# A four-tap shift filter moved wholly to TensorE, with 64-row tile pairs and a new written order

## The chip, the cores and the metric

The kernel runs on one core of a Trainium2 chip. The metric is the device time of one execution in microseconds (us). Before the change it is 241.32 us, the median of three runs (241.05 to 241.69). A separate execution was recorded by the hardware profiler; its span, from the first to the last instruction, is 238.8 us.

## What is computed

Two layers, each a long-convolution mixer (A) and an MLP (B), on 2048 positions of 512 channels in bf16:

```python
def _A_ref(q, k, v, shift_k, ssm_k, ssm_D):
    for t in range(ks):                       # ks = 4
        k_shift = k_shift + k_pad[:, t:t + S, :] * shift_k[:, ks - 1 - t][None, None, :]
    kv = k_shift * v
    ...
    y_f = kv_f * kf_f[None, :, :, :]          # rfft of kv and of ssm_k, both padded to 2S
    y = irfft2(y_f)[:, 0, :S, :]
    y = y + kv * ssm_D[None, None, :]
    return q * y
...
x = A_q
x = x + _A_ref(_layernorm(x), A_k, A_v, A_shift_k, A_ssm_k, A_ssm_D)
x = x + _B_ref(_layernorm(x), B_w1, B_b1, B_w2, B_b2)     # layernorm, gelu MLP, 512 -> 1376 -> 512
x = x + _A_ref(_layernorm(x), A_k, A_v, A_shift_k, A_ssm_k, A_ssm_D)
x = x + _B_ref(_layernorm(x), B_w1, B_b1, B_w2, B_b2)
```

The convolved signal y depends on k, v and the filters, not on x, so the kernel computes it once and uses it in both layers. The mixer A then costs only a layernorm, a product and a sum per layer.

## The kernel before, in words

**Stages.** The sequence is seen as 128 rows of 16 positions; the partition is the row. The Fourier transform is done by matmuls in two stages. "ht" transposes ssm_k (L528), "h1" is its first stage (L545, L547 in `stage1`), "h2" its second (L558, `stage2`). "fir" is the shift filter on k and the product with v, for four chunks of 128 channels; "x1" is the first stage for the result (`stage1` again), "x2" the second (L651, `products`), whose output is multiplied with the spectrum H (L450 by way of `tt`). "i1" (L674, `inverse1`) and "i2" (L731, `inverse2`) go back. Channels are cut in two halves (`PARTS`), and x2, i1 and i2 run per half, tagged `_0` and `_64`.

TensorE (PE) writes every tile to PSUM. `evac` (L453) copies it out, on ScalarE (ACT) or VectorE (DVE). A tile takes two of the eight PSUM banks in these stages, so four are open at a time. Between h2 and the products, 16 DMA copies swap partitions of H into a second array HS (L439, `ar<-ar`).

**The shift filter before.** Two chunks (0 and 1, `PE_CH`) go by `shift_pe`: 16 transposes of k (L589), an eviction into KT, then matmuls with diagonal tap matrices (L606; per chunk four groups of seven, 128 x 128 weights and 128 to 512 moving columns), and the product with v straight from PSUM (L613, on DVE). The other two chunks go by `shift_tt`: eight DVE instructions of 128 x 2048 each (four multiplications with the taps, three additions, the product with v; L450). For them k has three halo columns loaded by two further DMAs, and the taps are spread over partitions by a matmul (L511). The eight diagonal matrices are made on GpSimd (POOL, L520).

**The mixer and the MLP.** Layer 0 goes in nine blocks (`BLOCKS0`: 1, 1, then seven of 2 slices of 128 positions), layer 1 in four of 4. Per slice DVE takes statistics (L754, L756), normalizes (L768), multiplies with y and adds (L450); POOL computes the inverse root (L760, L762). The second layernorm's result z is transposed, by TensorE for the first two slices (L814) and by DMA for the others (L807), and goes through the MLP: L827 with gelu on ACT (L832), L860 (L849 for the last slice) with the sum on DVE (L864).

**The order.** Each engine runs a fixed queue. `Prog` collects operations with what they read and write; three tables written out by hand give the order of all operations (`ORDER`), which of the two engines takes an eviction (`SECOND`), and the PSUM banks (`BANKS`). `sync` derives the waits: an operation waits for its last producer, for readers of what it overwrites, and for the users of its PSUM banks. All loads, the HS copies and the DMA transposes but a few small ones are issued from one queue (SP), in order: a DMA whose wait is unmet holds back those behind it.

**Places.** One SBUF array `ar` is cut by hand. Before, the x1 output GX lies in R_4, where the h1 output G had been; k lies in R_K, and the MLP weight W1 and the table T2 are loaded over k later.

## Time and profile before

| | |
|---|---|
| median of three runs | 241.32 us |
| profiled execution, span | 238.8 us |
| runs minus span | 2.5 us |
| PE busy | 226.2 us (95%), 2312 instructions |
| DVE busy | 171.6 us (72%) |
| ACT busy | 138.3 us (58%) |
| POOL busy | 41.3 us (17%) |
| granted TensorE clock | 1.000 |
| DMA | 27.40 MB, 37035 packets |

Busy time is the time in which an engine had an instruction of the kernel in work. Matmuls are pipelined, so PE's duration of one (219 ns for 128 columns) is longer than the distance between two (about 56 ns); distances are read from the timeline. "Idle before, releaser" says how long an engine stood still ahead of a group and whose end let it go. Shares over the whole span mix stages that have different limits; here the first 83 us (Fourier stages) and the rest (mixer and MLP) are to be read apart.

### The profile page before, as it was taken

How to read it: one execution, taken by the hardware profiler on the slowest of the kernel's cores; microseconds unless marked ns; L12 is line 12 of the kernel's file. 1: busy time of each engine (PE TensorE's matmuls, PEld its weight loads, DVE VectorE, ACT ScalarE, POOL GpSimd, SP SyncE). 2: the span in 40 equal slices, each digit the busy share in tenths (PEclk: the TensorE clock that was granted, in tenths of full speed). 3: DMA queues.
4: the chain of work that ended last, by engine and by line, in shares of the span. 5: the costliest groups of instructions: out<-in, count | busy, mean ns of one | idle time of the engine just before them, and what ended most of it. 6: DMA issues, size and time to landing. Idle time of an engine off the chain costs nothing.

```text
span 238.8 us, 5555 instructions
## 1 busy us (share of the span) xinstructions
PE 226.2 (95%) x2312; PEld 151.6 (63%) x2332; DVE 171.6 (72%) x359; ACT 138.3 (58%) x225; POOL 41.3 (17%) x77
## 2 busy tenths in 40 slices
PE   7987989886999999999999999999999999999995
PEld 3875778875899886766766667644444444444543
DVE  0979999999999999999887999693793312030035
ACT  2598799999999995642754444342782042454100
POOL 2179000000013444041230310400220200000000
PEclk9999999999999999999999999999999999999999
DMA  6999949999960003111122022240013021310024
GB/s 241 364 342 383 383 148 253 249 272 309 379 227 0 3 0 68 26 23 31 37 47 44 0 48 44 45 88 3 0 22 66 3 44 31 101 44 3 0 71 148
DMA packets 37035, 27.40 MB, mean 115 GB/s; under 512 B 19506, under 2 KB 29969, under 8 KB 37010
## 3 DMA queue, kind: packets, MB, share of 16 engines
q1 hardware_dynamic: 36446, 26.91, 37.8%
q8 instruction: 18, 0.29, 0.5%
q10 hardware_dynamic: 564, 0.14, 0.4%
q14 instruction: 7, 0.06, 0.1%
HBM read 16.82 MB, written 2.10 MB: 79 GB/s over the span
## 4 chain that ended last, share of the span: by engine, by line
PE 77%; ACT 9%; DMA 4%; DVE 4%; SPq 3%; issue 3%; ACTq 0%
PE ps L860 31%; PE ps L827 30%; ACT ar L453 9%; PE ps L674 5%; PE ps L731 3%; SPq L439 3%; PE ps L545 3%; DMA ar<-in_A_ssm_k_dram 2%; DVE ar L453 2%; DMA ar<-ar 2%; PE ps L528 1%; PE ps L606 1%; PE ps L849 1%; DVE sm L754 1%; PE ps L589 1%
## 5 line engine op out<-in xcount | busy, mean ns | idle before, releaser
L832 ACT ACTIVATE ar<-ps,sm 128x256 bf16<-128x256 f32 (+4 forms) x143 | 64.7, 525 | 72.5 <-PE ps L827 68.1
L827 PE MATMUL ps<-ar 128*128 128x256 bf16 (+4 forms) x568 | 84.2, 297 | 0.2
L860 PE MATMUL ps<-ar 128*128 128x512 bf16 (+1 forms) x329 | 79.0, 379 | 0.6
L453 ACT ACTIVATE ar<-ps 128x1024 bf16<-128x1024 f32 (+1 forms) x81 | 72.5, 1057 | 9.0 <-PE ps L511 4.5
L827 PEld LDWEIGHTS ps<-ar 128*128 128x128 bf16 (+1 forms) x572 | 52.9, 100 | 29.8 <-ACT ar L832 0.5
L450 DVE TENSOR_TENSOR ar<-ar 128x512 bf16<-128x512 bf16 (+3 forms) x106 | 63.6, 634 | 2.0 <-DMA ar<-in_A_k_dram 1.3
L860 PEld LDWEIGHTS ps<-ar 128*128 128x128 bf16 (+1 forms) x341 | 33.1, 98 | 34.3 <-ACT ar L832 0.3
L864 DVE TENSOR_TENSOR ar<-ar,ps 128x512 bf16<-128x512 bf16 x31 | 20.6, 680 | 47.3 <-PE ps L860 47.3
L754 DVE BATCH_NORM_STATS2 sm<-ar 128x6 f32<-128x512 bf16 (+1 forms) x68 | 42.8, 647 | 0.1
L768 DVE TENSOR_SCALAR ar<-ar,sm 128x512 bf16<-128x512 bf16 x64 | 25.0, 407 | 7.8 <-POOL sm L762 5.2
L760 POOL TENSOR_SCALAR sm<-sm 128x2 f32<-128x2 f32 (+2 forms) x26 | 6.0, 232 | 93.9 <-DVE sm L756 93.3
L762 POOL TENSOR_TENSOR sm<-sm 128x2 f32<-128x2 f32 (+2 forms) x26 | 21.6, 832 | 2.2
L545 PE MATMUL ps<-ar 128*64 128x128 bf16 x512 | 17.1, 221 | 1.4 <-issue 0.8
L545 PEld LDWEIGHTS ps<-ar 128*64 128x64 bf16 x512 | 14.9, 110 | 3.2 <-issue 1.0
L674 PE MATMUL ps<-ar 128*128 128x128 bf16 x256 | 15.0, 220 | 0.6 <-ACT ar L453 0.6
L674 PEld LDWEIGHTS ps<-ar 128*128 128x128 bf16 x256 | 14.7, 114 | 0.8 <-ACT ar L453 0.8
L453 DVE CAST ar<-ps 128x1024 bf16<-128x1024 f32 x11 | 13.0, 1212 | 0.3 <-PE ps L558 0.3
L651 PE MATMUL ps<-ar 128*128 128x64 bf16 x256 | 9.8, 194 | 3.2 <-ACT ar L453 2.7
L453 DVE COPY ar<-ps 128x2048 bf16<-128x2048 bf16 (+1 forms) x8 | 8.2, 1024 | 6.4 <-PE ps L528 6.3
L651 PEld LDWEIGHTS ps<-ar 128*128 128x128 bf16 x256 | 8.2, 98 | 4.7 <-ACT ar L453 3.9
L756 DVE BATCH_NORM_AGGREGATE sm<-sm 128x2 f32<-128x6 f32 (+1 forms) x64 | 9.9, 171 | 0.3
L558 PE MATMUL ps<-ar 128*128 128x128 bf16 x128 | 8.6, 220 | 0.8 <-ACT ar L453 0.8
(34 smaller groups left out, 78.1 us busy)
## 6 DMA issues: line engine op xcount, KB each, us to landing
ar<-tab_s SPq DMA_DIRECT2D x16, 256.0 KB, 9.6
ar<-ar SPq DMA_DIRECT2D x16, 256.0 KB, 4.2
ar<-in_A_ssm_k_dram SPq DMA_DIRECT2D x4, 512.0 KB, 5.3
ar<-in_A_k_dram SPq DMA_DIRECT2D x8, 256.0 KB, 7.6
ar<-in_A_v_dram SPq DMA_DIRECT2D x8, 256.0 KB, 9.6
ar<-in_A_q_dram SPq DMA_DIRECT2D x4, 512.0 KB, 7.9
out_dram<-ar SPq DMA_DIRECT2D x7, 256.0 KB, 2.1
ar<-in_B_w_dram SPq DMA_DIRECT2D x1, 1376.0 KB, 12.6
```

The lines of the kernel that those rows point to most:

```text
L450: return P.op(eng, lambda e: e.tensor_tensor(o, a, b, op), reads=[a, b] + list(more), writes=[o])
L453: f = {ACT: lambda e: e.activation(dst, src(), AF.Copy), DVE: lambda e: e.tensor_copy(dst, src())}
L545: r = e.matmul(Q(tl, 64 * ri, 64, i * 128, [1, 128]), w, m, start=True, stop=True)
L651: r = e.matmul(Q(tl, 0, 128, i * pitch, [1, n]), w, m, start=True, stop=True)
L674: r = e.matmul(Q(tl, 0, 128, i * 128, [1, 128]), w, m, start=q == 0, stop=q == 1)
L754: P.op(DVE, lambda e, sj=sj, x=x: e.bn_stats(sj, x), reads=[x], writes=[sj])
L762: P.op(POOL, lambda e: e.tensor_tensor(r, v, hf, ALU.pow), reads=[v, hf], writes=[r])
L768: P.op(DVE, lambda e: e.tensor_scalar(o, x, m, r, ALU.subtract, ALU.mult), reads=[x, m, r], writes=[o])
L827: r = e.matmul(Q(tl, 0, rows, 0, [1, w]), a, m, start=dk == 0, stop=dk == 3)
L832: P.op(ACT, lambda e, dst=dst, tl=tl, rows=rows, bias=bias, w=w: e.activation(dst, Q(tl, 0, rows, 0, [1, w]), AF.Gelu_apprx_tanh, bias=bia ...
L860: r = e.matmul(Q(tl, 0, 128, 0, [1, 512]), ins[fc][0], ins[fc][1], start=fc == 0, stop=fc == 10)
L864: P.op(DVE, lambda e, x=x, tl=tl: e.tensor_tensor(x, x, Q(tl, 0, 128, 0, [1, 512]), ALU.add), reads=[x], writes=[x], tile=tl)
```

## The change

1. All four chunks of the filter go by matmul. `shift_tt`, the halo loads, the spreading of taps by a matmul and its two evictions are gone. KT has four buffers, k no halo.
2. The filter's matmuls take 64 rows each, in pairs: rows 0 to 63 and 64 to 127 of the same KT column block, each with its own diagonal (64 wide) and its own PSUM bank. Per chunk there are two halves of 22 matmuls with 64 to 256 moving columns, and two DVE products of 512 elements per half instead of one of 1024. The four diagonals are each made by one POOL multiplication of 128 x 256.
3. i1 likewise: per tile 32 matmuls of 64 rows and 64 columns instead of 16 of 128 and 128, and two evictions of 512 elements instead of one of 1024. The S2 table is permuted so that the pairs of d lie in one half of the partitions, and the table U halves.
4. GX of the first channel half is put where k was (R_K); the second half stays in R_4. W1 and three of the four T2 pieces, which lie over R_K, are loaded after x2 of the first half.
5. `ORDER`, `SECOND` and `BANKS` are new throughout: which engine evicts which tile, and the order on all queues, the DMA issues too. The loading of the gelu table comes after ACT's seventh eviction, so that a first table is loaded ahead of the first.

```diff
-PE_CH, PO_CH = (0, 1), ()
...
-    R_KT = (R_7, R_7 + 2080)
+    R_KT = (R_7, R_7 + 2080, R_6, R_6 + 2080)
...
-    R_GX, R_Z = R_4, R_4
+    R_Z = R_4
+    GX = {PARTS[0][0]: R_K, PARTS[1][0]: R_4 + 128 * PARTS[1][0]}
...
-    for i in range(4 * NPE):
-        o, t = A(0, 128, R_DG + i * 128, [1, 128]), M(0, 128, M_TAP + i, [1, 1])
-        P.op(POOL, lambda e, o=o, t=t: e.tensor_scalar(o, IDN, t, None, ALU.mult), reads=[IDN, t], writes=[o])
+    for c in range(4):
+        o = A(0, 128, R_DG + 256 * c, [64, 4], [1, 64])
+        tt(o, A(0, 128, R_FO, [0, 4], [1, 64]), A(0, 128, R_TC + 4 * c, [1, 4], [0, 64]), ALU.mult, POOL)
...
-        for a8 in range(2):
+        for a0 in (0, 8):
             tl = Tile(2)
             ins = []
-            for g in (2 * a8, 2 * a8 + 1):
-                for b in (0, 1, 2, 3, -1, -2, -3):
-                    j0, j1 = max(0, -b), min(3, 3 - b)
-                    ins.append((b, 512 * (g % 2) + 128 * max(b, 0), 128 * (j1 - j0 + 1),
-                                A(0, 128, R_KT[i] + (4 * g + b) % 16 * 130 + (2 if 4 * g + b >= 0 else 1), [1, 128]),
-                                A(0, 128, R_DG + (i * 4 + j0) * 128, [1, 128 * (j1 - j0 + 1)])))
+            for a in (0, 4, 1, 2, 3, 5, 6, 7, -1, -2, -3):
+                j0, j1 = max(0, -a), min(3, 7 - a)
+                k = R_KT[c] + (a0 + a) % 16 * 130 + (2 if a0 + a >= 0 else 1)
+                for r in range(2):
+                    ins.append((a, 512 * r + 64 * (a + j0), 64 * (j1 - j0 + 1), A(64 * r, 64, k, [1, 128]),
+                                A(64 * r, 64, R_DG + 256 * c + 64 * j0, [1, 64 * (j1 - j0 + 1)])))
...
-    def shift_tt(i):
-        c = DV_CH[i]
-        eng = POOL if c in PO_CH else DVE
-        acc, tmp = [A(0, 128, o, [128, 16], [1, 128]) for o in (R_TMP + 2048 * i, R_KV + 2048 * c)]
-        ...
-        tap(0, acc)
-        for j in range(1, 4):
-            tap(j, tmp)
-            tt(acc, acc, tmp, ALU.add, eng)
-        ...
+                for r, o, v in hs:
+                    x = e.tensor_tensor(o, Q(tl, 0, 128, 512 * r, [4, 16], [64, 8], [1, 4]), v, ALU.mult)
...
-                for q, r in enumerate((R_H, R_HS)):
-                    ins.append((i, q, A(0, 128, r + (dg // 4) * 512 + dg % 4, [4, 128]), A(0, 128, R_U + q * 128, [1, 128])))
+                for q, x in enumerate((R_H, R_HS)):
+                    for r in range(2):
+                        ins.append((i, q, r, A(64 * r, 64, x + (dg // 4) * 512 + dg % 4, [4, 128]),
+                                    A(64 * r, 64, R_U + q * 64, [1, 64])))
...
+            def by_act(e, zs=zs, src=src):
+                e.activation(zs[0], src(0), AF.Copy)
+                return e.activation(zs[1], src(1), AF.Copy)
...
+            P.op(BOTH, {ACT: by_act, DVE: by_dve}, writes=zs, tile=tl)
```

## The prediction

> **What bounds the kernel now.** I read the page's slices first, then the windows, the groups by shape, the timeline, and last the chain. The chain gives 61% of the span to the two mixer loops (L827, L860); the slices say when that begins.

> ```profile
> PE   7987989886999999999999999999999999999995
> DVE  0979999999999999999887999693793312030035
> ACT  2598799999999995642754444342782042454100
> ```

> A slice is 6 us. PE is full from the twelfth slice (66 us) to the end; before, it has holes while DVE and ACT are full. The windows (PE, PEld, DVE, ACT, POOL busy, clock, DMA share, GB/s) say it in us:

> ```profile
> 25.00:42.00 17.00, 15.80 (x263) 13.20 (x262) 16.65 (x15) 16.68 (x19) 0.00 (x0) 1.00 0.85 254
> 42.00:60.00 18.00, 14.47 (x400) 12.50 (x395) 18.00 (x17) 18.00 (x21) 0.00 (x0) 1.00 0.96 278
> 60.00:84.00 24.00, 23.45 (x366) 22.03 (x364) 23.38 (x55) 23.70 (x29) 6.04 (x16) 1.00 0.40 147
> ```

> From 25 to 84 us ACT and DVE empty PSUM, shift, and multiply without a pause. The mixer's first L827 starts at 83.08 and PE never waits again: 83.08 to the span's end, 238.8, is 155.7 us that the change leaves alone (L827, L860, L849 keep their instructions). So the change is worth what it moves that start, provided PE stays fed behind it. There the cover is thin:

> ```profile
> 88.39 19.60 SPq L807 DMA_TRANSPOSE ar<-ar  x6
> 92.50 4.09 PE L827 MATMUL ps<-ar 128*128 128x256 bf16 x36
> ```

> The third block's two transposes are issued at 88.39 and 89.74 and land 2.5 us later, at 92.2; PE takes them at 92.5. DVE computed them, and DVE had been busy since 6.04. Two accounts must therefore both get shorter: ACT's up to its last inverse eviction (84.75), and DVE's up to the second z2 norm (88.7).

> **Prices**, from the groups by shape:

> ```profile
> L453 ACT ACTIVATE ar<-ps 128x1024 bf16<-128x1024 f32 x75 | 69.8, 1091 | 4.2 <-PE ps L558 2.6 <-PE ps L545 1.5
> L450 DVE TENSOR_TENSOR ar<-ar 128x2048 bf16<-128x2048 bf16 x32 | 37.3, 1223 | 1.3 <-DMA ar<-in_A_k_dram 1.3
> L453 DVE CAST ar<-ps 128x1024 bf16<-128x1024 f32 x11 | 13.0, 1212 | 0.3 <-PE ps L558 0.3
> L864 DVE TENSOR_TENSOR ar<-ar,ps 128x512 bf16<-128x512 bf16 x31 | 20.6, 680 | 47.3 <-PE ps L860 47.3
> L613 DVE TENSOR_TENSOR ar<-ps,ar 128x1024 bf16<-128x1024 f32 x4 | 4.9, 1221 | 0.3 <-PE ps L606 0.3
> ```

> Back to back they overlap a little, so I use spacings: ACT 1024 wide 0.92 (23 in 21.22 us), 512 wide 0.49; DVE 2048 wide 1.16 (3 in 3.48), cast 1.14, PSUM multiply of 512 0.62 (4 L864 in 2.48).

> **ACT's account.** Before: 75 x 0.92 + 4 x 0.49 = 71 us of evictions after 9.61, and 3.8 of idle; 9.61 + 71 + 3.8 = 84.4, the trace's 84.75. In the changed order ACT holds 47 first-stage, second-stage and x2 tiles (43.2), one transpose eviction of 2048 (not in the trace; between one and two 1024s at full length, 0.92 to 2.18; I take two spacings, 1.84), 13 of the 16 i1 tiles, now two 512s each (0.92 to 1.24; two spacings, 0.98, so 12.7), i2 as before (7.5), and a second activation-table load that now stands after the seventh eviction (1.28, the row of the first one). Sum 66.5: 4.5 less. The 13 i1 tiles at 1.24 would cost 3.4 more; that goes to the range.

> **DVE's account.** Before: 6.04 to the last product at 68.2, 60.2 of work and 2.3 idle; then 20.0 to z2. Removed: 16 shift instructions x 1.16 = 18.6. Added: 16 PSUM multiplies of 512 for 4 of 1024, 16 x 0.62 - 4 x 1.14 = 5.4 (between 0.61 and 0.68 each); one more transpose eviction, 1.2; the new order also gives DVE 13 first-stage/x2 and 4 second-stage evictions where it had 9 (9.1 more), and one more small statistic. Up to the last product that is 58.1, 2.1 less. After it: 3 i1 tiles at 1.24 (0.83 to 1.36 by the 512-wide copy and multiply) for 2 at 1.14, but three statistics fewer ahead of z2: 17.8, 2.2 less. Sum 4.3 less. The diff frees DVE alone; it is the new order that shares it with ACT.

> **What eats into it.** (1) Idle. Sixteen shift instructions needed only k and taps, so DVE always had work; now everything DVE and ACT do up to the products waits for a PE tile. Following the changed order tile by tile, ACT starts 1.4 earlier (8.2, since h1 follows the first ht tile), but waits 4.7 in five pieces before its first h2 tile, 0.8 in the h2 stretch and 1.1 where i1 of the second half needs the last product: 6.6 for 3.8. ACT's end: 8.2 + 66.5 + 6.6 = 81.3, 3.4 earlier. DVE waits 2.4, then 0.6: 6.04 + 58.1 + 2.4 + 17.8 + 0.6 = 84.9, 3.8 earlier.

> (2) PE. k transposes double: 32 x 0.056 = 1.8 more. The filter: four chunks of two halves instead of two chunks of four. A half is now 22 matmuls, 11 pairs; a pair lies on two 64-row tiles and streams 2048 columns in all per row tile: 0.88 if the pair overlaps, 1.76 if not (one half before: 14 matmuls, 4096 columns, 1.7). Row pairs are nowhere in this trace. The nearest row is the column pair of L545:

> ```profile
> 38.44 0.61 PE L558 MATMUL ps<-ar 128*128 128x128 bf16 x8
> 38.98 0.64 PE L545 MATMUL ps<-ar 128*64 128x128 bf16 x16
> 39.55 0.62 PE L558 MATMUL ps<-ar 128*128 128x128 bf16 x8
> ```

> Sixteen half-wide matmuls take what eight whole ones do, 0.45: the pair overlaps fully, and I take that for rows too, so the filter stays at 7.0 in all. i1 falls from 0.89 a tile to 0.47, hidden: its eviction (0.98) was already as long. The same rows show the cost of changing shapes: 38.44 to 38.98 and 38.98 to 39.55 are 0.54 and 0.57 for 0.45 of streaming, so about 0.12 a change. The old order has 14 such changes ahead of the mixer, the new one 37: 23 x 0.12 = 2.8 us of PE. Most falls where PE waits anyway; I charge 1.1, the part that falls into stretches where ACT or DVE wait for PE.
> [...]

> (3) Queues. The halo loads go (0.8 us of DMA time), so the last table lands about 32 instead of 33.49, and its tile wants it at 32.2: covered, barely. With half the spectrum in k's place, three T2 pieces and W1 now wait for x2 of the first half, and on SP's queue the last H-to-HS copies stand behind T2, q and W2. SP issues in 0.65, copies land 0.87 apart, W2 takes 4.9 (54 to 64 in the old trace): the last copy lands near 60.7, its product is due near 62. W1, last, lands near 68 and is due at 79. Cost nothing; without the cover it is rival C. POOL's eight diagonals (9.2) become four multiplies of 256 (between 0.42 and 3.5 each); the first is due at 20 us, the second at 29: covered by h1.

> **Sum.** The later account decides: 3.4 - 1.1 = 2.3 us. Span 238.8 - 2.3 = 236.5; the runs take 2.5 more than the profiled span (241.32 against 238.8): **239.0 us**. Block three then: PE is there at 80.8 + 9.4 = 90.2, z2 at about 89; PE stays fed.

> **Rivals.**
> A. *No new idle.* If ACT waits no more than the old 3.8 and the shape changes hide, ACT gains 4.5 + 1.4 = 5.9 and DVE 4.3; the smaller holds: 241.3 - 4.3 = 237.0 (235.4 if z2 has slack that I do not see). For it: PE has room, 14.47 of 18 at 42 to 60. Against: every hand-over between PE and its two emptiers is now in series.
> B. *Hand-over idle takes all.* Another 2 us in the first 40 us, where PE (15.80 of 17) is nearly full as well, and nothing moves: 241.2, inside 0.3%.
> C. *Row pairs do not overlap* (slower). Every half costs 1.76: four more of 0.88 before the second stage ends, 3.5, with PE's load there at 19.9 in the 18 us it has (7.0 filter, 7.1 second stage, 3.6 x1, 0.9 transposes, 1.3 changes), and four more behind. It delays the H-to-HS copies and with them the products. Charged 4.0 net: 239.0 + 4.0 = 243.0. It decides from a pair that takes 1.6 times as long as one of its matmuls (2.3 of the 4.0). For it: no row shows row pairs; i1's strided weights load in 113 ns against 98. Against: L545.
> [...]
> D. *A late DMA.* If the q piece that the first statistics wait for (the old ones took 5 to 12 us to land) or the last copy comes 3 us late, DVE loses it whole: 241.5 to 242.

> **Chances.** Forecast 0.47, A 0.15, B 0.15, C 0.15, D 0.08. 0.3% (0.7 us) is about what can be told from no change. Faster: forecast and A and a little of B, 0.64; same: B and half of D, 0.18; slower: C and the rest, 0.18. The range takes in A, some way into its lower end, and reaches C's price: 236.0 to 243.0.

> **What would show it.** Right: pairs of filter and i1 matmuls 2 to 4 ns apart, a filter half near 0.9; last second-stage eviction near 38 to 39 (was 41.4); last product near 67; first mixer matmul near 80.8; PE full from there. Wrong: a half at 1.76 (C); PE holes behind 81, above all ahead of the third block (z2 late); DVE waiting for in_A_q or ar<-ar around 52 to 62 (D); ACT idle above 7 us (B).

## The result and the profile after

The changed kernel takes **248.89 us** (median of four, 248.64 to 250.13) against 241.30 for the kernel before beside it: a ratio of 1.031, 95% interval 1.028 to 1.034. I had forecast 239.0 (236.0 to 243.0). The profiled execution took 250.13 us with a span of 248.3; it is the slowest of the four, the others took 248.64 to 249.00. Ratios, and the median of one run below, leave out a few executions that ran longer at a lower clock (one took 376.64 us at 0.576).

The page of the changed kernel, slices of 6.2 us (busy tenths; PEclk is the granted clock):

```profile
PE   5988899986747999999999999989999999999996
DVE  0897789999737999999989899962887731200423
ACT  2177889996948997381554372345364242455000
PEclk9999999997985999999999999999999999999999
```

Where TensorE (PE) was full from the twelfth slice on, it now has a hole in slices ten to thirteen (56 to 81 us, digits 6747); VectorE (DVE) and ScalarE (ACT) have one beside it in the twelfth (3 and 4), and the clock falls in the tenth, twelfth and thirteenth. The windows that the prediction showed of before (PE, PEld, DVE, ACT, POOL, clock, DMA share, GB/s), for the changed kernel:

```profile
25.00:42.00 17.00, 15.81 (x344) 14.31 (x341) 14.16 (x15) 15.32 (x17) 0.00 (x0) 1.00 0.69 201
42.00:60.00 18.00, 14.18 (x385) 12.83 (x382) 17.97 (x22) 16.49 (x18) 0.38 (x1) 0.97 0.94 281
60.00:84.00 24.00, 17.78 (x620) 16.04 (x617) 17.16 (x27) 18.69 (x33) 3.75 (x7) 0.81 0.48 163
```

From 60 to 84 us PE is idle for 6.2 of 24 us, DVE for 6.8 and ACT for 5.3; before, all three were full. What PE waited for, 20 to 80 us (total, times, longest):

```profile
PE ps L631 <- issue: 4.7, 2, 3.4
PE ps L606 <- issue: 1.8, 1, 1.8
PE ps L631 <- DVE ar L444: 1.4, 1, 1.4
PE ps L606 <- ACT ar L447: 1.2, 1, 1.2
PE ps L575 <- issue: 1.1, 1, 1.1
```

"issue" means that PE waited for nothing that the profile shows: no buffer, no engine, no transfer of data. L631 is the inverse's first stage in pairs, L606 the second stage of x, L575 the filter. The timeline of PE there shows where it stops:

```profile
59.29 2.15 PE L606 MATMUL ps<-ar 128*128 128x64 bf16 x37 [1.82 <-issue]
...
62.96 0.89 PE L631 MATMUL ps<-ar 64*128 64x64 bf16 x42
65.13 1.09 PE L631 MATMUL ps<-ar 64*128 64x64 bf16 x54 [1.29 <-issue]
...
68.09 0.35 PE L631 MATMUL ps<-ar 64*128 64x64 bf16 x10
71.88 1.17 PE L631 MATMUL ps<-ar 64*128 64x64 bf16 x54 [3.44 <-issue]
72.98 1.04 PE L606 MATMUL ps<-ar 128*128 128x64 bf16 x16
```

The stop of 3.44 us falls inside a tile: 10 of its 32 matmuls run, 22 come 3.44 us later (with the next 32: x54). Nothing in the program stands between them. In the last line a tile of 16 takes 1.04 us where it took 0.64 at 66.15; the granted clock there is 0.50.

**What stops it.** Counting PE's instructions from the start (matmuls, weight loads, sequencer's), the stops come after 705, 961, 2241, 2497 and 2753, always 449 plus a multiple of 256. The trace also has the packets of the queue "q8 instruction", 16 KB each, 21 of them here and 18 before. Each time PE goes on 1.4 to 1.5 us after such a packet has ended. In quiet stretches a packet starts about when PE has come to within 256 instructions of the boundary (0.5 us after that at 77.04; in the mixer up to 2.6 us before it); beside much data it starts later. I call that moment "asked". The waits counted from it are estimates, good to some tenths of a us where 256 instructions take 3 to 6 us:

| kernel | boundary | asked | packet starts | ends | PE stops, goes on |
|---|---|---|---|---|---|
| before | 705 | 15.60 | 19.54 | 20.66 | 20.77, 22.08 |
| changed | 2241 | 51.39 | 56.80 | 57.80 | 57.47, 59.29 |
| changed | 2497 | 59.29 | 62.67 | 63.77 | 63.85, 65.13 |
| changed | 2753 | 65.13 | 69.40 | 70.49 | 68.44, 71.88 |

All such stops sum to 8.3 us in the changed kernel, 2.1 before. The longer of the two before (the first row of the table) lies inside a group of 16 transposes:

```profile
22.08 1.01 PE L589 MATMUL ps<-ar 128*128 128x128 bf16 x15 [1.31 <-issue]
```

So PE runs out of instructions: the pairs double what it takes per tile of the inverse, and the packets wait 3.4 to 5.4 us while q, T2, W2 and W1 move (339 to 365 GB/s between 54 and 66 us).

The losses, by the traces: the mixer loops start at 90.46 instead of 83.08 (7.4 later), and last 155.6 us from first to last matmul instead of 153.3 (2.3 longer). Together that is 9.7 us, more than the 7.6 between the medians; one reason is that the profiled execution lies 1.2 us above its median.

### The profile page after: what moved, and what is told of

Read it like the earlier page. It is cut to its first block, busy times and chain, and to the rows that moved or that the text cites. A ratio compares the mean times of both kernels' runs of the same rounds, so it can differ in the third digit from the quotient of the medians.

```text
span 248.3 us, 6388 instructions
## 1 busy us (share of the span) xinstructions
PE 227.6 (92%) x2738; PEld 152.1 (61%) x2738; DVE 175.0 (70%) x370; ACT 134.0 (54%) x229; POOL 33.6 (14%) x70
## 4 chain that ended last, share of the span: by engine, by line
PE 44%; DVE 29%; ACT 13%; issue 5%; DMA 4%; POOL 3%; SPq 0%; ACTq 0%
PE ps L825 16%; PE ps L792 16%; ACT ar L447 11%; DVE sm L719 10%; DVE ar L444 6%; DVE ar L733 4%; DVE ar L447 4%; PE ps L631 3%; POOL sm L727 3%; DVE ar L829 2%; PE ps L606 2%; DVE sm L721 2%; DMA ar<-ar 2%; DMA ar<-tab_small 2%; PE ps L528 2%
## 5 line engine op out<-in xcount | busy, mean ns | idle before, releaser
L792 PE MATMUL ps<-ar 128*128 128x256 bf16 (+5 forms) x572 | 81.8, 297 | 1.1 <-DMA ar<-ar 0.6
L447 ACT ACTIVATE ar<-ps 128x1024 bf16<-128x1024 f32 (+2 forms) x58 | 54.3, 1024 | 19.2 <-PE ps L515 10.2
L444 DVE TENSOR_TENSOR ar<-ar 128x512 bf16<-128x512 bf16 (+3 forms) x92 | 46.6, 521 | 7.3 <-ACT ar L447 6.6
L829 DVE TENSOR_TENSOR ar<-ar,ps 128x512 bf16<-128x512 bf16 x31 | 20.6, 678 | 41.9 <-PE ps L825 41.9
L447 DVE CAST ar<-ps 128x1024 bf16<-128x1024 f32 x17 | 20.2, 1213 | 2.1 <-PE ps L528 1.1
L631 PE MATMUL ps<-ar 64*128 64x64 bf16 x512 | 11.9, 209 | 6.2 <-issue 4.7
L631 PEld LDWEIGHTS ps<-ar 64*128 64x128 bf16 x512 | 10.8, 118 | 7.1 <-issue 5.1
L447 DVE COPY ar<-ps 128x2048 bf16<-128x2048 bf16 (+1 forms) x9 | 9.4, 1041 | 8.1 <-PE ps L498 7.2
L606 PE MATMUL ps<-ar 128*128 128x64 bf16 x256 | 10.9, 204 | 3.2 <-issue 1.8
L606 PEld LDWEIGHTS ps<-ar 128*128 128x128 bf16 x256 | 9.5, 105 | 4.1 <-issue 1.9
L585 DVE TENSOR_TENSOR ar<-ps,ar 128x512 bf16<-128x512 f32 x16 | 10.0, 682 | 1.2 <-PE ps L575 1.2
```

Source lines behind the costliest of these rows:

```text
L444: return P.op(eng, lambda e: e.tensor_tensor(o, a, b, op), reads=[a, b] + list(more), writes=[o])
L447: f = {ACT: lambda e: e.activation(dst, src(), AF.Copy), DVE: lambda e: e.tensor_copy(dst, src())}
L606: r = e.matmul(Q(tl, 0, 128, i * pitch, [1, n]), w, m, start=True, stop=True)
L631: o = e.matmul(Q(tl, 0, 128, 512 * r + i * 64, [1, 64]), w, m, start=q == 0, stop=q == 1)
L792: r = e.matmul(Q(tl, 0, rows, 0, [1, w]), a, m, start=dk == 0, stop=dk == 3)
L829: P.op(DVE, lambda e, x=x, tl=tl: e.tensor_tensor(x, x, Q(tl, 0, 128, 0, [1, 512]), ALU.add), reads=[x], writes=[x], tile=tl)
```

## The experiments

**Theory 1**: the instruction supply, as above. **Theory 2**: the new written order, whatever the queues hold. **Theory 3**: hand-overs among the three engines. **Rival 4**: the pairs themselves (a half-idle PE would lose its clock). Ratios are to the kernel before, run beside each, with their 95% intervals.

**Take the data away: W1 and W2 late.**

```diff
-    dma(W1 ...)
-    dma(W2 ...)
+    dma(W1 ..., reads=GATE)      # GATE: what the last first-stage inverse tiles write
+    dma(W2 ..., reads=GATE)      # both moved behind those tiles in ORDER
```

> The changed kernel, with W1, W2 and W2's tail issued behind the last first-stage inverse tile and waiting for it (2.75 MB less in the queues between 52 and 72 us). Theory 1 (TensorE runs out of instructions: in the changed kernel it stops after 2241, 2497 and 2753 instructions, that is every 256, and goes on 1.4 us after a packet of the instruction queue that had waited 3.4 to 5.4 us behind data): those packets wait 2 to 3 us, the stops of 1.82, 1.29 and 3.44 us shrink to under 2.5 us in sum, first mixer matmul 86.5 to 88 for 90.46, time 245 to 247. Theory 2 (the written order of the tiles, whatever the queues hold): the stops and the time stay, 248 to 250. Theory 3 (hand-overs among TensorE, ScalarE and VectorE): stays, or later by 1 to 3 us if the mixer now waits for W1.

Measured: 245.66 us, ratio 1.0142 (1.0068 to 1.0216). PE's timeline of this kernel (L590 is the inverse's first stage, L565 the second stage of x):

```profile
60.98 0.36 PE L590 MATMUL ps<-ar 64*128 64x64 bf16 x10 [0.20 <-ACT ar L406]
62.57 1.09 PE L590 MATMUL ps<-ar 64*128 64x64 bf16 x54 [1.23 <-issue]
...
66.25 1.63 PE L590 MATMUL ps<-ar 64*128 64x64 bf16 x64
67.81 0.64 PE L565 MATMUL ps<-ar 128*128 128x64 bf16 x16
```

The packets for 2241, 2497 and 2753 waited 2.1, 2.9 and 1.1 us (5.4, 3.4, 4.3), and of 6.5 us of stops in these stages 1.23 are left, at the one boundary whose packet still waited 2.9. The 6.5 is a high mark, though: in the profiles of three runs below that keep the pairs and W1 and W2 among these tiles (the table first, and the former mixer order, whole and from the last inverse tile on) there is no stop at 2241, and the other two sum to 4.5 to 4.9 us. In the run with the table first (same lines) they are:

```profile
62.41 1.09 PE L590 MATMUL ps<-ar 64*128 64x64 bf16 x54 [1.04 <-issue]
...
69.15 1.09 PE L590 MATMUL ps<-ar 64*128 64x64 bf16 x54 [3.43 <-issue]
```

What the late loads surely removed is the stop at 2753: its packet waited 1.1 us here and 4.0 to 4.3 in those four, and the stop there was 2.2 to 3.4 us. The mixer starts at 87.15, and has lost 1.9 us to W1, which now lands late. Theory 1 holds, and theory 2 does not for these stops: the same tiles in the same order stop far less once these loads are gone.

**Take the instructions away: full rows.**

```diff
-                    for r in range(2):
-                        ins.append((i, q, r, A(64 * r, 64, ...), A(64 * r, 64, R_U + q * 64, [1, 64])))
+                    ins.append((i, q, A(0, 128, ...), A(0, 128, R_U + q * 128, [1, 128])))   # U block-diagonal
```

> The changed kernel, with the inverse's first stage in full rows again: per tile 16 matmuls of 128 rows and 128 columns for 32 of 64 rows and 64 columns, same order, same two evictions of 512. 256 matmuls and 256 weight loads less, twice the streaming (0.89 for 0.47 us a tile). Theory 1: two stops fewer in this stage, the 1.29 and the 3.44 us go or shrink to under 1.5 in sum, time 244 to 247. Rival (the pairs do what they are for, and the new order is what costs): the stage gets longer by up to 16 x 0.4 us where TensorE sets its pace, time 249 to 253.

Measured: 244.78, ratio 1.0129 (1.0050 to 1.0208). The stage's group in this kernel:

```profile
L633 PE MATMUL ps<-ar 128*128 128x128 bf16 x256 | 15.5, 219 | 2.0 <-DVE ar L448 1.3 <-issue 0.4 <-ACT ar L643 0.3
```

Here the data stay: the packet for 2753 waited 3.6 us (4.3). But PE takes 8.3 us over the 256 instructions ahead of that boundary (3.1), and finds the next ones there. Issue costs this stage 0.4 instead of 4.7, the clock is 1.00 throughout, and the mixer starts at 84.63. With the run above: it takes dense instructions and queued data together. Theory 3 has no part in these stops, which wait for no engine.

**The table first.** Operation 0 before 2 in `ORDER`.

> The changed kernel, with the small table issued first on ScalarE's queue and ssm_D's row third. In the changed kernel the table is issued at 1.30 us and its first user starts at 5.98, 1.2 later than before. If the first 40 us are a chain from there, the time falls by 0.8 to 1.3 us (247.6 to 248.1); if VectorE's and ScalarE's waits for k and for TensorE absorb it, by less than 0.4.

Measured: 248.24, ratio 1.0271 (1.0170 to 1.0372), not to be told from the changed kernel (1.028 to 1.034). Inconclusive by itself; a cleaner run follows.

**The pairs put into the kernel before**, and two controls.

> The kernel before, with the inverse's first stage alone in pairs of 64-row tiles: 32 matmuls of 64 columns a tile, two evictions of 512, row order of the stage's table to match; filter and sequence as before. 256 more matmuls and weight loads. Theory 1: in the stage TensorE takes 256 instructions in about 4 us, while a packet of instructions needs 2.7 of waiting, 1.1 of transfer and 1.4 until use; stops of 0.5 to 1.5 us at each of four packets between 57 and 80 us, time 242.5 to 245. Rival (pairs are harmless, the new order costs): 241 to 242, the two narrower evictions on ScalarE included.

```diff
# e5: the same count without pairs
-   A(64 * r, 64, x ..., [4, 128]), A(64 * r, 64, R_U + q * 64, [1, 64])
+   A(0, 128, x ..., [4, 128]), A(0, 128, R_U + q * 128 + r * 64, [1, 64])
# e6: 16 matmuls of 128 columns as before, and the two evictions of 512
```

> The kernel before, with the inverse's first stage in full rows, but each matmul of 128 columns cut into two of 64: 32 matmuls and 32 weight loads a tile, as in the run with pairs, but streaming 0.89 us a tile, two evictions of 512. Theory 1 (the number of instructions costs): the same 256 matmuls and weight loads more as with pairs, stops at 2497 and 2753 instructions again, time within 1 us of the 243.96 of the pairs. Rival 4 (the pairs themselves cost: half-idle TensorE, the clock falls to 0.5 when it has less to do): no stops over 0.5 us, clock 1.00, 241.3 to 242.3.

> The control: the kernel before, with the inverse's first stage in 16 matmuls of full rows a tile as it was, but two evictions of 512 for one of 1024 (and the row order of the pairs). The prediction priced a pair of 512s at 0.98 for 0.92: 16 x 0.06, 0.7 us on ScalarE and 0.1 on VectorE, so 241.5 to 242.3. All theories expect that; above 243 the evictions, and not instructions or pairs, explain the run with pairs.

Measured: pairs 243.96, ratio 1.0089 (1.0051 to 1.0127); halves 245.35, 1.0145 (1.0073 to 1.0218); control 242.73, 1.0046 (1.0006 to 1.0086). The stage's groups, pairs:

```profile
L677 PE MATMUL ps<-ar 64*128 64x64 bf16 x512 | 11.9, 207 | 4.1 <-issue 2.9 <-ACT ar L454 1.1
```

halves:

```profile
L681 PE MATMUL ps<-ar 128*128 128x64 bf16 x512 | 17.9, 198 | 2.1 <-issue 1.1 <-ACT ar L458 0.9
```

and control:

```profile
L679 PE MATMUL ps<-ar 128*128 128x128 bf16 x256 | 15.4, 220 | 0.6 <-ACT ar L458 0.6
```

With 512 matmuls PE waits for issue, in pairs or not; with 256 it does not. In the halves the clock is 1.00 in this stage, so rival 4 is not needed for the stops. But the sizes are not cleanly separated: the intervals of pairs and control overlap, and by the middle values half of what the pairs cost is the price of the two evictions (0.46 of 0.89%). Two forecasts missed by a little: the control lies 0.4 us above its range, and the halves 1.4 us from the pairs, not within 1, with one stop (1.07 us, at 2497) where I had expected two. The halves also carry 2.5 us more of busy PE (17.9 for 15.4), which I had put at nothing.

**Is it the count, or the place in the work?** 64 short matmuls more in the warm-up of the changed kernel.

```diff
+        for i in range(64):
+            r = e.matmul(Q(tl, 0, 128, 0, [1, 64]), z[:, :128], z[:, :64], start=True, stop=True)
```

> The changed kernel with 64 matmuls of 64 columns more in the warm-up at its start, 128 instructions of TensorE, while it waits for the first table anyway. Theory 1: TensorE still stops only after 705, 961, 2241, 2497 or 2753 of its instructions, counted from the start, so each stop falls 64 matmuls earlier in the work than before, and goes on 1.3 to 1.6 us after a packet of the instruction queue. Any theory of a missing buffer, tile or transfer: the stops stay at the same work, that is at 128 instructions more.

One run, 252.74. Its timeline (L608 second stage of x, L633 inverse):

```profile
61.95 0.47 PE L608 MATMUL ps<-ar 128*128 128x64 bf16 x10 [0.26 <-ACT ar L643]
65.29 0.34 PE L608 MATMUL ps<-ar 128*128 128x64 bf16 x6 [2.87 <-issue]
...
69.21 0.47 PE L608 MATMUL ps<-ar 128*128 128x64 bf16 x10
71.76 0.34 PE L608 MATMUL ps<-ar 128*128 128x64 bf16 x6 [2.08 <-issue]
```

These stops cut tiles of the second stage of x (10 and 6 of 16 matmuls), where in the changed kernel the last two had cut tiles of the inverse, and they come after 2753 and 3009 instructions; at the same work they would have come after 2625 and 2881. PE goes on 1.33 and 1.36 us after the packets' ends. The count decides where PE stops. That this kernel is 4 us slower is another matter, below.

**The mixer's order.** `ORDER`, `SECOND` and `BANKS` of the mixer's operations taken from the kernel before, for all of them (alone, then with full rows and table):

> The changed kernel, with the operations of the mixer (statistics, norms, transposes, the two matmul loops) in the relative order and on the banks that they had before; everything ahead of them in the new order. From the mixer's first matmul to its last it is 153.3 us before and 155.6 in the changed kernel, also where that starts 3 to 6 us earlier. If the written order of the mixer costs this, the mixer returns to 153.3 to 154.0 and the time falls by 1.5 to 2.3, to 246.5 to 247.4. If VectorE's lateness costs it (last product 76.3 for 68.2), it stays, and the time is 248.5 to 250.

> The changed kernel with three edits at once: inverse's first stage in full rows, small table first, mixer in its former order. What is left of the change is the filter in row pairs on TensorE, and the new sequence ahead of the mixer. If the three costs add: 248.9 less 4.1 (full rows), less 0.6 (table), less 1.5 to 2.3 (mixer order): 241.9 to 242.7. If the filter on TensorE saves what the prediction thought, 2 us below the kernel before: 239 to 240.

Measured: 249.21, ratio 1.0278 (1.0193 to 1.0363), and 250.80, 1.0383 (1.0294 to 1.0471): both forecasts missed. The mixer itself did return to 154.1 and 153.4 us, with VectorE's last product as late as 76.3 and 75.0; so the written order does make its 1.5 to 2.2 us. But the edit took more ahead of the mixer, which starts at 91.16 and 92.58. The waits of VectorE, 55 to 78 us, in the second of the two:

```profile
DVE sm L674 <- DMA ar<-in_A_q_dram: 4.0, 2, 3.8
DVE ar L599 <- PE ps L586: 2.0, 1, 2.0
```

A statistic of a q piece that lands late now stands ahead of the last products. I then kept the new order up to the last second-stage inverse tile, and up to the third block:

> As the run with three edits, but the mixer's operations follow the former order only from where the last second-stage inverse tile stands; ahead of that the new order is kept, so that no statistic of a late q piece stands in front of VectorE's last products (it waited 4.0 us for one there). If the costs add: 248.9 less 4.1 (full rows), 0.6 (table) and 2.2 (mixer order): 242.0, range 241.3 to 242.8; so the filter on TensorE and the sequence ahead of the mixer are worth nothing against the kernel before. If VectorE's lateness costs the mixer its 2.2: 243.8 to 244.6. If the filter gains: below 240.8.

> The changed kernel with its pairs kept in filter and inverse: small table first, mixer in its former order from the last second-stage inverse tile on, W1 issued behind the last q piece, W2 behind the last first-stage inverse tile and waiting for it. Theory 1: with 1.38 MB less among the data of 52 to 64 us the stops in the inverse's first stage sum to 1 to 3 us (6.5 in the changed kernel), and with table and mixer order 242 to 244. If the queues don't matter: 246 to 247.

> The changed kernel with the mixer in its former order from where the last second-stage inverse tile stands, and nothing else. From the mixer's first matmul to its last 153.3 to 154.1 us instead of 155.6, time 246.5 to 247.4, if the written order of the mixer costs it; 155.0 to 155.8 and 248.5 to 249.5 if VectorE's lateness ahead of it does.

Measured: 246.98 (1.0196, 1.0138 to 1.0254), 249.60 (1.0283, 1.0209 to 1.0358), 249.73 (1.0332, 1.0272 to 1.0391). All three missed: the two orders meet badly, and PE has three holes of 2.9 us in sum in the mixer's first 8 us, each the same in all three. They say nothing of the later blocks. With W2 late, and W1 still among the tiles, the stops at 2497 and 2753 were 1.23 and 2.90 us, the waits of the packets 2.9 and 3.7: W2 alone is too little.

**The rest, and the shift once more.**

> The changed kernel with the inverse's first stage in full rows and the small table first; mixer as in the changed kernel. If table and full rows add: 244.8 less 0.6 to 1.2, 243.6 to 244.2, first mixer matmul at 83.4 for 84.63. If the table's 1.2 us are absorbed: 244.5 to 245.

> The kernel before with 64 matmuls of 64 columns more in its warm-up, 128 instructions, in time that TensorE spends waiting for the first table. Theory 1: boundaries after 449 and 705 instructions fall 64 matmuls earlier in the work, the first packet is asked for while TensorE idles; the stops of 1.01 and 1.54 us become about 0 and 0.2 to 0.8, and the time falls by 0.5 to 1.8 us, to 239.6 to 241.0. If those stops are covered by VectorE and ScalarE, which are busy there: within 0.4 us of 241.5.

> The run before with the 64 short matmuls more in the warm-up. Theory 1: the stop of about 1.4 us near 21 us shrinks below 0.5; time 242.5 to 243.8, 0.5 to 1.2 below its neighbour without them. If where the boundaries fall is worth nothing: the same as the neighbour within 0.4.

> The run before with the mixer's operations in the former order from behind the third block on. If the written order of the later blocks makes the holes near 57 and 73 us after the mixer's start: mixer 153.4 to 154.2 us, time 1 to 2 below its neighbour, 241 to 242.5. If VectorE, later by its share of evictions, makes them: mixer 155 to 156 and no gain.

Measured: full rows and table 244.47, ratio 1.0142 (1.0106 to 1.0178), first mixer matmul 84.38, mixer 155.6: the table is worth nothing, it is absorbed. Kernel before, shifted: 243.68 (1.0099, 1.0075 to 1.0122), a miss: the 64 matmuls do not fit into the idle start, VectorE's first operation comes at 9.23 for 6.04. Full rows, table, shifted: 248.41 (1.0299, 1.0270 to 1.0329); with the former order behind the third block 249.85 (1.0364, 1.0328 to 1.0400), holes of 3.3 and 0.7 us in the mixer. Both missed: with the shift the stop near 21 us did go (the 16 transposes there take 1.20 us in one piece), but the mixer lasts 159.2 us. So no version here beats the kernel before. Whether a shift that costs nothing would gain was not tried.

## Why the prediction was wrong, point by point

**The step that failed** is (2) of "What eats into it", with (3). I counted PE's cost of the new tiles as streaming plus 0.12 us a change of shape, 2.8 in all and 1.1 charged, and said that the faster inverse tile is hidden behind its eviction. That PE must also be supplied with 406 matmuls and 406 weight loads more was in no term. (The two profile pages differ by 426 matmuls, but the trace of before has 20 matmuls less than weight loads; the control, which has as many of both as the kernel before, shows 2332 of each.) "Queues: cost nothing" looked only at when the last copy and W1 land (64.8 and 72.5, later than the 60.7 and 68 that I gave), not at the instruction packets behind the same data. The trace of before had shown such a stop: 1.31 us of issue inside L589 at 20.77, behind a packet that had waited 3.9. The price: 4.1 us by the medians of the changed kernel and the run with full rows. By the mixer's start it is 5.8 (84.63 for 90.46), but there the profiled executions lie 1.2 us above and 0.5 below their medians. The clock of 0.50 behind the stops (3.4 and 6.8 us of it) is part of this price; its share was not separated.

**"155.7 us that the change leaves alone"** failed by 2.3: the loops keep their instructions, but not their order. It is 155.6 from first to last matmul in the changed kernel, with full rows, and with full rows and table, whether they start at 90.46, 84.63 or 84.38. The chain, first of before and then of the changed kernel, runs through VectorE now, where it had been PE:

```profile
PE 77%; ACT 9%; DMA 4%; DVE 4%; SPq 3%; issue 3%; ACTq 0%
PE 44%; DVE 29%; ACT 13%; issue 5%; DMA 4%; POOL 3%; SPq 0%; ACTq 0%
```

That the order causes it is what the two runs with the former order show (154.1 and 153.4), with one reservation: their mixers also start later, and none of them kept what it won, so part of the time may only have moved ahead of the start. Which operation in the order does it is not settled.

**The filter gives less than I said even without the stops in the inverse.** With full rows and table the mixer starts at 84.38, not 80.8. VectorE's work up to the last product was right: 58.3 for 58.1. Its idle time was not: 4.4 for 2.4 up to there and 2.5 for 0.6 behind it (2.0 of that waiting for PE's full-row tiles). It starts 0.5 late. These sum to 4.4, where 3.6 are to be explained. Most of this is rival B, hand-overs, about as large as its price of 2 us, twice; two stops of 0.9 and 0.6 us fall in the same stretch, ahead of 29 us, but the kernel before has 2.1 us of them there too.

**ACT's account** had decided the forecast, with an end 3.4 us earlier. It was right in one price: a pair of 512s takes 0.97 (0.98). In the changed kernel its waits cannot be compared with the forecast's 6.6, since 5.6 us of them are for L606, between stops. With full rows and table they can: ACT starts at 8.8 (8.2), works 68.3 (66.5) and waits 8.5 (6.6), and its last inverse eviction ends at 85.6, where I had said 81.3 and the kernel before has 84.76. So this account wins nothing even where the inverse does not stop, and its waits pass the 7 us that I had named as the sign of B. Part of the missing work is that I took the spacing of 0.92 for every eviction: one that stands alone takes 1.02.

**Rival C was wrong, and the step behind the forecast right.** Two filter halves of the changed kernel:

```profile
44.22 1.94 PE L575 MATMUL ps<-ar 64*128 64x256 bf16 x44
```

The second half starts 0.89 after the first (0.88 forecast, 1.76 without overlap), and the two matmuls of a pair start 3 to 4 ns apart. So the overlap is full here. The forecast failed elsewhere.

**Rival D**, a late DMA, did not happen to the data: in the changed kernel VectorE has no wait for q or the H copies up to its last product. It happened to instructions.

## What to carry to other kernels

Count TensorE's instructions in a stage, not only its columns: before halving tiles, look for "issue" in its waits and for idle time inside a tile, and compare how long it takes 256 instructions with the wait of an instruction packet in that stage, plus 2.5 us (here about 1.1 for the packet and 1.4 until TensorE went on). In the changed kernel dense pairs were cheap where the queues were quiet (from 72 to 85 us packets waited 0.5 to 1.7 us, 256 instructions took 4 to 5 us, and TensorE did not stop) and dear where loads were queued. Moving the loads took away part of the stops there; taking instructions out of the inverse took away those in the inverse. A written order that is good for one timing can lose in another, and the old order grafted on the new one lost at the seam in all three trials.

## What the runs showed of the hardware

```profile
DVE ar L735 <- DMA ar<-ar: 2.5, 1, 2.5
```

  The same stands at 147.35 in the changed kernel (4.1 us, packet at 149.31). The 18 traces together have 540 transposes: of the 85 with an instruction packet under way within 2.5 us of their issue, 61 took over 3.0 us to land, and of the other 455 only 7 did. That is a strong coincidence; no run moved a packet to test it as the cause. It may explain part of the shifted runs' mixers of 159.4 and 159.2 us.
